# Sparse attention with two expert layers: attention's outputs without an f32 copy, two early weight pieces in place of eight, and the late leaky ReLU on two engines

## Chip, cores, metric

One core of a Trainium2 chip runs the whole program as one launch. The metric is the device time of a launch in microseconds, the median of several runs.

## What is computed

Three layers follow one another (batch 4, 8 heads, 576 positions, head size 64; 2304 tokens of 512 values):

```python
def _attn_ref(q, k, v):             # window 32; heads 4 to 7 dilated by 4
    scores = scale * np.matmul(q, k.transpose(0, 1, 3, 2))
    scores = np.where(masks[None], scores, -1e9)
    attn = np.exp(scores - np.max(scores, axis=-1, keepdims=True))
    attn = attn / (np.sum(attn, axis=-1, keepdims=True) + 1e-09)
    return np.matmul(attn, v)
def _moe_ref(x, w_in, w_out, alpha):   # 512 -> 2048 -> 512, w_in and w_out given as float64
    h = x @ w_in
    g = np.maximum(h, 0.0) + alpha * np.minimum(h, 0.0)
    return g @ w_out
def _moe2_ref(x, w_gate, w1, w2):      # 8 experts, 512 -> 1024 -> 512
    P = ...                            # exp of the gate's logits, 8 Sinkhorn rounds
    for e in range(E):
        out += P[:, e:e+1] * (np.maximum(x @ w1[e], 0.0) @ w2[e])
```

## The kernel before

**Numbers in two parts.** Nearly every matmul works on a value split into a high part (rounded to the matmul's f32r form) and a low part (value minus high part); `three` (lines 377 to 380) gives three matmuls: high with high, high with low, low with high. The splitting of every operand costs an ACT cast for the high part and a subtraction on DVE or POOL for the low one.

**Attention** (`att_S`, `att_E`, `att_R`, `att_X`, `att_V`) works through 16 groups, four to a batch, one group two heads. The sequence of the first four is written out by hand in `opening()`; `attention()` yields the later ones step by step. `att_V` puts the group's result, in PSUM bank `pv`, into the token tile `XS`: ACT casts the high part (line 271, or 282 for the dilated heads), ACT copies the same columns as f32 to `xst` (272, 284), and DVE subtracts for the low part (`low_part`, line 146, emitted later by `flush`). Then SyncE stores `xst` to a DRAM tile `x32[b]` (lines 275 and 287; groups 0 and 1 of a batch pass both lines). After it, `after()` issues the load of v for the group two further on. All DMAs go out on SyncE's queue, in order.

**The first expert layer, plain part.** A unit is 288 tokens (chunk c) by 256 hidden columns; `run` merges the first layer of one unit (`m1_L1`) with the second layer of the unit before (`m1_L2`). `m1_L1` leaves a column tile in PSUM; the leaky ReLU is two DVE instructions (lines 396 and 399), then ACT casts (400) and POOL subtracts (401). Two side lists are stepped between them by credit: `aside` for attention, `wside` for the conversion of weights. Nine units run so (`units[:hand]`).

**Weights from float64.** `from_double` (512 columns a piece) makes f32 values out of the two words of a float64: an absolute value on ACT (521), five DVE instructions (522, 526, 530, 532, 536), then POOL. Eight of the pieces which the *fast* part needs first are converted in this early stage (`early`, EARLY = 8, from unit 4 on, EARLY_AT) and stored to DRAM tiles `wd`.

**The planned part.** `second` lists operations with their engines, costs and due times, and `arrange` plans them: at each time the engine takes the ready operation with the earliest due time, and the due time of an operation is pulled ahead of all those that wait for it. The outcome is a fixed order on each engine. It begins with seven plain units; then the first expert layer's other 1536 hidden columns follow in 12 fast blocks (v = 0 to 11; a batch of tokens by 512 columns, seven products of block matrices in place of eight for layer one, `m1_layer1`; `m1_layer2` for the second). Then the gate, Sinkhorn, and the second expert layer.

- `m1_tokens(b)` makes the four sums T1 to T4 of a batch's tokens: it loads `x32[b]` (line 1200) into a `raw` slot, forms the sums by adds, and splits them into `x` slots.
- `m1_weights(v0)` makes the weights' sums for one column block: for the first block (fi = 1) it loads the `wd` pieces (lines 1144 and 1153); for the later ones it loads the float64 words and calls `double`, the planner's form of the conversion, six DVE instructions with PSUM bank SW[1] as scratch (1080, 1089, 1098, 1105, 1114 and an add).
- The strips of `XS` that hold a batch's tokens are handed to other uses by `release` once their readers are done (`strip_place`); a release has due time 0, so what must come before it is planned early. The strip b12 of batch 0 becomes a place for hidden values (class "h").
- The leaky ReLU in this part runs on two engines: ACT makes relu(-x) (1020, 1284), DVE joins it with `rest` = 1 - alpha (1013, 1279).

Of the kernel before, what the change touches and what calls it, by code (L numbers as in the profile page):

```python
# [58 lines left out]
def program(tc, qk, v, moe_w_in, moe_w_out, moe_alpha, moe2_w_gate, moe2_w1, moe2_w2, masks, out):  # L59
# [8 lines left out]
    x32 = [spill.tile([P, KD, 2 * CH], F32, name=f"x32b{b}") for b in range(B)]  # L68
# [36 lines left out]
    xst = attc.tile([P, 2, 2 * CH], F32, name="xst")  # L105
# [142 lines left out]
    def att_V(i):  # L248
# [6 lines left out]
        for g in range(2):  # L255
# [11 lines left out]
            if g == 0:  # L267
                whole = xst[:, i % 2]
            if p < 2:
                c = 2 * b + g  # L270
                nc.scalar.copy(xh(c, p), pv[:, :CH])
                nc.scalar.copy(whole[:, g * CH : (g + 1) * CH], pv[:, :CH])
                low_part(nc.vector, xl(c, p), pv[:, :CH], xh(c, p))
                if g:
                    nc.sync.dma_start(x32[b][:, p], whole)
                continue
            for cc in range(2):
# [6 lines left out]
            nc.scalar.copy(  # L284
                whole.rearrange("p (j r) -> p r j", r=4)[:, 2 * g : 2 * g + 2], pv[:, :CH].rearrange("p (r j) -> p r j", r=2)
            )
        nc.sync.dma_start(x32[b][:, p], whole)
# [84 lines left out]
    made = [0]  # L372

# [8 lines left out]
    def m1_L1(n, c, st):  # L382
        ah, al = wa_of[n]
        for t in range(FS // P):
            ps = bank("psH")
            cols = slice(t * P, (t + 1) * P)
            for kk in range(KD):
                three(
                    ps[:, :CH], ah[:, kk, cols], al[:, kk, cols], xh(c, kk), xl(c, kk), kk == 0, kk == KD - 1
                )  # L390
            ft = st * (FS // P) + t
            k = made[0]
            made[0] += 1
            gh, gl = gview(k % 4)
            u = GU[:, k % 2]
            nc.vector.tensor_scalar(
                out=u, in0=ps[:, :CH], scalar1=0.0, scalar2=alpha[:, ft : ft + 1], op0=ALU.min, op1=ALU.mult
            )
            nc.vector.scalar_tensor_tensor(out=u, in0=ps[:, :CH], scalar=0.0, in1=u, op0=ALU.max, op1=ALU.add)
            nc.scalar.copy(gh, u)  # L400
            nc.gpsimd.tensor_tensor(out=gl, in0=u, in1=f(gh), op=ALU.subtract)
            gt[c, st, t] = (gh, gl)
            yield
# [58 lines left out]
    EARLY = 8  # L462
# [86 lines left out]
    class Side:  # L549
# [5 lines left out]
        def add(self, g, steps, due):  # L555
            self.q.append([g, steps, due])
# [242 lines left out]
    def second(last, plain):  # L799
# [42 lines left out]
        def dma(kb):  # L842
            return [("SP", kb / 290.0)]
# [111 lines left out]
        def strip_place(b, n):  # L955
            plan = (("h", 1), ("h", NF - 1), ("x", 2), ("x", 3))[b]
            if b > 1 and n != "b12":
                plan = ("zz", 0)
            x = XS[:, 8 * 2 * CH * b : 8 * 2 * CH * (b + 1)].rearrange("p (t h k w) -> p t h k w", t=2, h=2, k=2)
            return Place(lambda: x[:, int(n[2]) - 1, :, int(n[1]) - 1], [plan], block_done[b])  # L960
# [226 lines left out]
        def m1_tokens(b, prio):  # L1187
# [8 lines left out]
            for n in ("T2", "T3", "T1", "T4"):  # L1196
                xo[b, n] = Slot("x", (n, b), b)
            add(
                dma(1180),
                lambda _: nc.sync.dma_start(rawv(r)[:, : KD * 2 * CH].rearrange("p (k c) -> p k c", k=KD), x32[b]),  # L1200
                prio - 15,
                (),
                [(r, i) for i in range(4)],
            )
# [734 lines left out]
        before = last  # L1939
        release([("xs", 0, "b12")], 0, [strip_place(0, "b12")])  # L1940
        m1_tokens(0, TF - 20)
        m1_weights(0, TF - 25, sF(1))
        for i, unit in enumerate(plain):
# [13 lines left out]
        for v in range(NF):  # L1957
            b = batch(v)
            if v < B - 1:
                m1_tokens(v + 1, sF(v + 1) - 15)  # L1960
# [46 lines left out]
    with tc.manual_schedule():  # L2007
# [22 lines left out]
        EARLY_AT = 4  # L2030
# [101 lines left out]
```

## Time and profile before

| | us |
|---|---|
| median of 3 runs | 1990.39 (1990.17 to 1993.63) |
| the profiled execution | 1992.63 |
| its span, first to last instruction | 1990.9 |
| TensorE busy | 1939.9 (97%) |
| VectorE (DVE) busy | 1449.8 (73%) |
| ScalarE (ACT) busy | 1031.5 (52%) |
| GpSimd (POOL) busy | 549.7 (28%) |

The profile is of one execution; its page gives shares over the whole span, so the stages, which have different limits, are read from tables by stretch, from the timeline of an engine, and from the list of what each engine waited for. SPq is SyncE's queue, which issues the DMAs. The granted clock is a mean over a stretch, as a share of 2.4 GHz.

### The profile page before, as it was taken

The page shows a single profiled execution, that of the slowest core. Times are in us where ns is not written, and L with a number is a line of the kernel's source. Part 1 is how long each engine was busy: PE and PEld are TensorE (multiplying, and loading weights), DVE is VectorE, ACT ScalarE, POOL GpSimd, SP SyncE. Part 2 cuts the span into 40 slices and gives each one's busy share as a digit, 9 for nine tenths or more (in the row PEclk, how much of TensorE's full clock was granted, in tenths as well). Part 3 has the DMA queues.
Part 4 walks back from the last instruction along what each step waited for, and adds up shares of the span by engine and source line. Part 5 has one row for each costly group of instructions (what it writes and reads, how often), then busy time and mean ns, then how long its engine had stood idle before and what let it go on. Part 6 is the DMA issues. An engine that isn't in the chain of part 4 may idle for free.

```text
span 1990.9 us, 36935 instructions
## 1 busy us (share of the span) xinstructions
PE 1939.9 (97%) x14629; PEld 1912.9 (96%) x14629; DVE 1449.8 (73%) x2223; ACT 1031.5 (52%) x1915; POOL 549.7 (28%) x413
## 2 busy tenths in 40 slices
PE   6888989999999999999999999999999999999999
PEld 5777989999999999999999999999999999999998
DVE  5686588644657788887967778867776667767776
ACT  6754667666754555645546445534444434444442
POOL 3443253111236545454622112412110101101100
PEclk7998999999999999999999999999999999999999
DMA  7545563718565577867588668677678766666662
GB/s 256 172 144 207 210 221 126 258 54 277 187 215 213 199 256 255 290 244 278 219 329 284 238 207 319 230 285 238 232 272 298 245 209 223 236 212 224 235 214 87
DMA packets 126749, 452.75 MB, mean 227 GB/s; under 512 B 13936, under 2 KB 23920, under 8 KB 121072
## 3 DMA queue, kind: packets, MB, share of 16 engines
q1 hardware_dynamic: 126576, 450.39, 64.9%
q8 instruction: 115, 1.88, 0.4%
q14 instruction: 58, 0.48, 0.1%
HBM read 313.50 MB, written 136.84 MB: 226 GB/s over the span
## 4 chain that ended last, share of the span: by engine, by line
PE 91%; DVE 4%; DMA 2%; ACT 1%; issue 0%; SPq 0%; DVEq 0%; ACTq 0%
PE W L378 8%; PE W L380 8%; PE W L379 8%; PE SW L380 8%; PE SW L379 8%; PE SW L378 8%; PE SX L380 7%; PE SX L378 7%; PE SX L379 7%; PE X L380 6%; PE X L378 6%; PE X L379 6%; PE psS L189 1%; DMA RAW<-in_moe_w_out 1%; PE psV L260 1%; DMA v<-in_v 1%
## 5 line engine op out<-in xcount | busy, mean ns | idle before, releaser
L378 PE MATMUL W<-XS,WT 128*128 128x384 f32 (+1 forms) x936 | 308.2, 329 | 1.5 <-DVE acc L422 0.6
L380 PE MATMUL W<-XS,WT 128*128 128x384 f32 (+1 forms) x936 | 307.2, 328 | 1.3 <-DVE WT L593 1.3
L379 PE MATMUL W<-XS,WT 128*128 128x384 f32 (+1 forms) x936 | 307.3, 328 | 0.0
L1889 DVE SCALAR_TENSOR_TENSOR oR<-SW,pt,oR 128x256 f32<-128x256 f32 x363 | 170.0, 479 | 121.3 <-PE SW L380 119.6
L1889 DVE SCALAR_TENSOR_TENSOR oR<-SX,pt,oR 128x256 f32<-128x256 f32 x351 | 167.6, 480 | 80.9 <-PE SX L380 80.5
L380 PE MATMUL X<-XS,WT 128*128 128x384 f32 (+1 forms) x660 | 218.4, 331 | 0.8 <-DVE WT L593 0.8
L378 PE MATMUL X<-XS,WT 128*128 128x384 f32 (+1 forms) x660 | 218.6, 331 | 0.0
L379 PE MATMUL X<-XS,WT 128*128 128x384 f32 (+1 forms) x660 | 218.2, 331 | 0.0
L378 PEld LDWEIGHTS W<-XS,WT 128*128 128x128 f32 x936 | 176.2, 188 | 2.7 <-DVE acc L422 0.9
L380 PEld LDWEIGHTS W<-XS,WT 128*128 128x128 f32 x936 | 175.7, 188 | 1.6 <-DVE WT L593 1.6
L379 PEld LDWEIGHTS W<-XS,WT 128*128 128x128 f32 x936 | 175.9, 188 | 0.0
L593 POOL TENSOR_TENSOR WT<-rawR,WT 128x512 fp32r<-128x512 f32 (+1 forms) x60 | 79.6, 1332 | 251.5 <-ACT WT L1555 165.5
L593 POOL TENSOR_TENSOR WT<-RAW,WT 128x512 fp32r<-128x512 f32 (+1 forms) x57 | 78.0, 1370 | 257.2 <-ACT WT L1555 113.5
L1679 ACT CAST hR<-WX 128x768 fp32r<-128x768 f32 x127 | 104.3, 834 | 74.8 <-DVE WX L1755 65.9
L593 DVE TENSOR_TENSOR hR<-WX,hR 128x768 fp32r<-128x768 f32 x126 | 141.2, 1129 | 1.9 <-ACT hR L1679 1.7
L593 DVE TENSOR_TENSOR XS<-WX,XS 128x768 fp32r<-128x768 f32 (+1 forms) x117 | 122.5, 1048 | 18.6 <-ACT XS L1286 18.3
L593 POOL TENSOR_TENSOR wR<-rawR,wR 128x512 fp32r<-128x512 f32 x39 | 53.2, 1365 | 269.5 <-ACT wR L1555 154.7
L380 PEld LDWEIGHTS X<-XS,WT 128*128 128x128 f32 x660 | 123.9, 188 | 1.7 <-DVE WT L593 1.5
L378 PEld LDWEIGHTS X<-XS,WT 128*128 128x128 f32 x660 | 124.1, 188 | 0.2
L379 PEld LDWEIGHTS X<-XS,WT 128*128 128x128 f32 x660 | 124.0, 188 | 0.0
L1745 ACT ACTIVATE WX<-WX 128x768 f32<-128x768 f32 x48 | 40.6, 847 | 155.1 <-DVE WX L593 155.1
L593 POOL TENSOR_TENSOR wR<-RAW,wR 128x512 fp32r<-128x512 f32 x39 | 52.6, 1351 | 243.8 <-ACT wR L1555 156.7
(337 smaller groups left out, 6352.3 us busy)
## 6 DMA issues: line engine op xcount, KB each, us to landing
RAW<-in_moe_w SPq DMA_DIRECT2D x20, 1024.0 KB, 6.6
rawR<-in_moe_w SPq DMA_DIRECT2D x19, 1024.0 KB, 6.3
WT<-a11g SPq DMA_DIRECT2D x33, 512.0 KB, 4.5
WT<-S2g SPq DMA_DIRECT2D x33, 512.0 KB, 4.5
WT<-a12g SPq DMA_DIRECT2D x33, 512.0 KB, 3.7
WT<-S3g SPq DMA_DIRECT2D x33, 512.0 KB, 3.5
WT<-S1g SPq DMA_DIRECT2D x33, 512.0 KB, 3.6
WT<-a22g SPq DMA_DIRECT2D x33, 512.0 KB, 4.9
```

Source lines behind the costliest of these rows:

```text
L189: nc.tensor.matmul(ps[half(hh), bk, at : at + KB], x[half(hh), 0, j * QB : (j + 1) * QB], x[half(hh), 1, key_start(j) : key_start(j) + KB] ...
L260: nc.tensor.matmul(pv[half(hh), lo - g * CH : hi - g * CH], vt[:, j, hh * D : (hh + 1) * D], at[:, j, hh * QB + lo - j * QB : hh * QB + hi ...
L378: nc.tensor.matmul(ps, lh, rh, start=start, stop=False, skip_group_check=more)
L379: nc.tensor.matmul(ps, lh, rl, start=False, stop=False, skip_group_check=more)
L380: nc.tensor.matmul(ps, ll, rh, start=False, stop=stop, skip_group_check=more)
L593: eng.tensor_tensor(out=out, in0=x, in1=y, op=op)
L1679: add(act(n2), lambda _: nc.scalar.copy(hv(h[n])[:, 0], tm[i]), prio, [("t", i)], [(h[n], "h")])
L1745: add(act(n2), lambda _: nc.scalar.activation(tm[1], tm[1], AF.Relu), t + 1, [("t", 1)], [("t", 1)])
L1889: nc.vector.scalar_tensor_tensor(out=o, in0=x, scalar=p_, in1=o, op0=ALU.mult, op1=ALU.add)
```

## The change

- `att_V` no longer copies the result as f32 and no longer stores it; the tiles `xst` and `x32` are gone.
- `m1_tokens` rebuilds a batch's tokens as high part plus low part, four adds (on DVE or POOL) from `XS` into the `raw` slot, in place of the load. It is called for all batches ahead of the plain units (batch 0 still first); the release of batch 0's strip b12 moves behind batch 0's, and that strip first serves the class "x" (token sums of era 0), then "h" as before.
- EARLY is 2, not 8, and the early pieces begin at unit 6, not 4. The six others are converted by `double` in the planned part: two of the first matrix, all four of the second.
- From the ninth column tile on (BUSY = 8, so from unit 4), `m1_L1`'s leaky ReLU is relu(-x) on ACT and one join on DVE.

```diff
@@ att_V
-            if g == 0:
-                whole = xst[:, i % 2]
             if p < 2:
                 c = 2 * b + g
                 nc.scalar.copy(xh(c, p), pv[:, :CH])
-                nc.scalar.copy(whole[:, g * CH : (g + 1) * CH], pv[:, :CH])
                 low_part(nc.vector, xl(c, p), pv[:, :CH], xh(c, p))
-                if g:
-                    nc.sync.dma_start(x32[b][:, p], whole)
                 continue
...
                 nc.scalar.copy(ho, src)
                 low_part(nc.vector, lo, src, ho)
-            nc.scalar.copy(
-                whole.rearrange("p (j r) -> p r j", r=4)[:, 2 * g : 2 * g + 2], pv[:, :CH].rearrange("p (r j) -> p r j", r=2)
-            )
-        nc.sync.dma_start(x32[b][:, p], whole)
@@ m1_L1
+            if k < BUSY:
                 ...
+            else:
+                nc.scalar.activation(u, ps[:, :CH], AF.Relu, scale=-1.0)
+                nc.vector.scalar_tensor_tensor(
+                    out=u, in0=u, scalar=rest[:, ft : ft + 1], in1=ps[:, :CH], op0=ALU.mult, op1=ALU.add
+                )
@@
-    EARLY = 8
+    EARLY = 2
@@ strip_place
+            plan = [plan]
+            if (b, n) == (0, "b12"):
+                plan = [("x", 0), *plan]
@@ m1_tokens
-            add(
-                dma(1180),
-                lambda _: nc.sync.dma_start(rawv(r)[:, : KD * 2 * CH].rearrange("p (k c) -> p k c", k=KD), x32[b]),
-                prio - 15,
-                (),
-                [(r, i) for i in range(4)],
-            )
+            for i, n in enumerate(("b11", "b12", "b21", "b22")):
+                x = xs_view(b, n)
+                add(
+                    flex(n2),
+                    lambda e, i=i, x=x: sub(E3[e], blk(i), f(x[:, 0]), f(x[:, 1]), ALU.add),
+                    prio - 2,
+                    [("xs", b, n)],
+                    [(r, i)],
+                )
@@ second
+        m1_tokens(0, TF - 20)
         release([("xs", 0, "b12")], 0, [strip_place(0, "b12")])
-        m1_tokens(0, TF - 20)
         m1_weights(0, TF - 25, sF(1))
+        for b in range(1, B):
+            m1_tokens(b, sF(b) - 15)
...
-            if v < B - 1:
-                m1_tokens(v + 1, sF(v + 1) - 15)
@@
-        EARLY_AT = 4
+        EARLY_AT = 6
```

## Rows read from the trace of the kernel before

**Rows 1.** The page: busy time of TensorE, and its granted clock in forty slices.

```profile
PE 1939.9 (97%) x14629; PEld 1912.9 (96%) x14629; DVE 1449.8 (73%) x2223; ACT 1031.5 (52%) x1915; POOL 549.7 (28%) x413
...
PEclk7998999999999999999999999999999999999999
```

**Rows 2.** Table by stretch: length, busy PE, PEld, DVE, ACT, POOL, clock, DMA share, GB/s.

```profile
20.00:52.00 32.00, 23.47 (x311) 19.61 (x312) 19.88 (x42) 21.67 (x87) 10.14 (x7) 0.69 0.63 210
52.00:124.00 72.00, 68.24 (x918) 60.86 (x917) 53.99 (x108) 49.10 (x154) 33.15 (x26) 0.98 0.53 170
124.00:190.40 66.40, 51.34 (x452) 46.44 (x446) 52.35 (x98) 31.86 (x89) 26.72 (x21) 0.82 0.46 149
190.40:234.00 43.60, 43.57 (x328) 43.57 (x329) 20.59 (x37) 23.64 (x57) 12.20 (x11) 1.00 0.57 212
234.00:258.70 24.70, 18.52 (x132) 17.38 (x131) 20.31 (x31) 15.88 (x31) 9.38 (x6) 0.99 0.72 271
```

**Rows 3.** Timeline of TensorE: start, length, instruction, idle time before and its releaser.

```profile
171.42 0.40 PE L378 MATMUL psY<-GP,WT 128*128 128x288 f32 x1 [2.52 <-DVE GU L399]
...
177.37 0.44 PE L380 MATMUL psY<-GP,WT 128*128 128x288 f32 x1
```

**Rows 4.** Groups on DVE, 124 to 190 us: count, busy us, mean ns, idle before.

```profile
L536 DVE SCALAR_TENSOR_TENSOR RAW<-RAW 128x512 f32<-128x512 uint32 x9 | 6.2, 686 | 0.2
...
L396 DVE TENSOR_SCALAR GU<-psH,alpha 128x288 f32<-128x288 f32 x8 | 4.1, 513 | 3.0 <-PE psH L380 3.0
L399 DVE SCALAR_TENSOR_TENSOR GU<-psH,GU 128x288 f32<-128x288 f32 x8 | 3.7, 458 | 0.3
```

**Rows 5.** Groups on ACT, 0 to 190 us.

```profile
L284 ACT COPY xst<-psV 128x288 f32<-128x288 f32 x16 | 11.9, 745 | 0.0
```

**Rows 6.** Groups on DVE, 0 to 190 us.

```profile
L146 DVE TENSOR_TENSOR XS<-psV,XS 128x144 fp32r<-128x144 f32 x32 | 11.7, 415 | 14.6 <-ACT xst L284 14.6
```

**Rows 7.** Timeline of all engines, 33 to 47 us.

```profile
37.61 1.29 ACT L237 COPY at<-psX 96x512 f32<-96x512 f32 x3
...
37.84 0.33 SPq L287 DMA_DIRECT2D x32b<-xst  x1
...
38.26 0.39 SPq L132 DMA_DIRECT2D v<-in_v  x1
...
42.77 2.40 PE L260 MATMUL psV<-at,v 96*64 96x64 f32 x40 [4.63 <-DMA v<-in_v]
```

**Rows 8.** Instructions on tile WX alone, 126.5 to 186 us: DVE, ACT, POOL.

```profile
126.50:186.00 59.50, 23.60 (x32) 5.45 (x8) 11.58 (x9) 0.83 0.47 151
```

**Rows 9.** Groups on DVE, 186 to 262 us.

```profile
L1013 DVE SCALAR_TENSOR_TENSOR WX<-WX,rest,W 128x288 f32<-128x288 f32 x7 | 3.6, 513 | 8.9 <-ACT WX L1020 8.9
```

**Rows 10.** Groups on DVE, 255 to 400 us; then line 1080: ns, first and last start.

```profile
L1114 DVE SCALAR_TENSOR_TENSOR RAW<-RAW,MIDF 128x512 f32<-128x512 uint32 x16 | 12.8, 800 | 0.3
...
L1080 DVE TENSOR_SCALAR SW<-RAW 128x512 uint32<-128x512 uint32 x16 | 11.1, 692 | 0.4
...
L1080 DVE TENSOR_SCALAR SW<-RAW x16: 681/695/697, 260.1 to 373.8; 128x512 uint32<-128x512 uint32 x16
```

**Rows 11.** Timelines of SyncE's queue and of DVE behind 190 us.

```profile
203.55 1.28 SPq L1200 DMA_DIRECT2D MIDF<-x32b  x1
...
219.80 1.11 DVE L593 TENSOR_TENSOR MIDF<-MIDF 128x576 f32<-128x576 f32 x1
```

**Rows 12.** Timelines of TensorE, DVE and POOL, 246 to 258 us.

```profile
257.43 0.40 PE L379 MATMUL SW<-XS,WT 128*128 128x288 f32 x1 [4.38 <-DVE XS L593]
...
251.68 3.15 DVE L1279 SCALAR_TENSOR_TENSOR WX<-WX,rest 128x288 f32<-128x288 f32 x2
...
251.49 4.60 POOL L593 TENSOR_TENSOR MIDF<-MIDF 128x576 f32<-128x576 f32 x3
```

**Rows 13.** Adds of 128x576: on DVE (255 to 400 us), on POOL (186 to 262 us).

```profile
L593 DVE TENSOR_TENSOR MIDF<-MIDF 128x576 f32<-128x576 f32 x4 | 3.0, 750 | 0.0
...
L593 POOL TENSOR_TENSOR MIDF<-MIDF 128x576 f32<-128x576 f32 x6 | 9.2, 1540 | 7.7 <-PE W L380 6.9 <-DVE MIDF L593 0.7
```

More of the change, by code (lines that the diff above doesn't have):

```diff
@@ L67, in program @@
     spill = pool(es, "spill", space=bass.MemoryType.DRAM)
-    x32 = [spill.tile([P, KD, 2 * CH], F32, name=f"x32b{b}") for b in range(B)]
     py = pool(sp, "py", bufs=2, space=PSUM)
@@ L104, in program @@
     eye = attc.tile([P, P], BF16, name="eye")
-    xst = attc.tile([P, 2, 2 * CH], F32, name="xst")
     def load_consts():
@@ L372, in program @@
     made = [0]
+    BUSY = 8
     def gview(k):
@@ L395, in m1_L1 @@
             u = GU[:, k % 2]
-            nc.vector.tensor_scalar(
-                out=u, in0=ps[:, :CH], scalar1=0.0, scalar2=alpha[:, ft : ft + 1], op0=ALU.min, op1=ALU.mult
-            )
-            nc.vector.scalar_tensor_tensor(out=u, in0=ps[:, :CH], scalar=0.0, in1=u, op0=ALU.max, op1=ALU.add)
+            if k < BUSY:
+                nc.vector.tensor_scalar(
+                    out=u, in0=ps[:, :CH], scalar1=0.0, scalar2=alpha[:, ft : ft + 1], op0=ALU.min, op1=ALU.mult
+                )
+                nc.vector.scalar_tensor_tensor(out=u, in0=ps[:, :CH], scalar=0.0, in1=u, op0=ALU.max, op1=ALU.add)
+            else:
[3 more added lines that the diff above has]
+                )
             nc.scalar.copy(gh, u)
@@ L958, in strip_place @@
                 plan = ("zz", 0)
+            plan = [plan]
+            if (b, n) == (0, "b12"):
+                plan = [("x", 0), *plan]
             x = XS[:, 8 * 2 * CH * b : 8 * 2 * CH * (b + 1)].rearrange("p (t h k w) -> p t h k w", t=2, h=2, k=2)
-            return Place(lambda: x[:, int(n[2]) - 1, :, int(n[1]) - 1], [plan], block_done[b])
+            return Place(lambda: x[:, int(n[2]) - 1, :, int(n[1]) - 1], plan, block_done[b])
         def wt_place(i, cls):
@@ L1197, in m1_tokens @@
                 xo[b, n] = Slot("x", (n, b), b)
-            add(
-                dma(1180),
-                lambda _: nc.sync.dma_start(rawv(r)[:, : KD * 2 * CH].rearrange("p (k c) -> p k c", k=KD), x32[b]),
-                prio - 15,
-                (),
-                [(r, i) for i in range(4)],
-            )
+            for i, n in enumerate(("b11", "b12", "b21", "b22")):
[6 more added lines that the diff above has]
+                    [(r, i)],
+                )
             def total(at, x, y):
```

## Prediction

> **What bounds the kernel now.** The page's busy shares come first: TensorE is busy 1939.9 us of the span, 97%, so about 51 us is all that idling costs, and its clock row is below 9 only in the first slices [rows 1]. What a change outside TensorE's own work can win therefore lies early. The table by stretches says where [rows 2]: from 20 to 52 us TensorE is busy 23.47 of 32.00 at a granted clock of 0.69, from 52 to 124 us 68.24 of 72.00, from 124 to 190.4 us only 51.34 of 66.40 at 0.82, then, the work having been handed over to the planned order, 43.57 of 43.60, and from 234 to 258.7 us 18.52 of 24.70. Behind that I expect nothing of these edits.
>
> Idle time has a second price, the clock. After the wait of 2.52 us that ended at 171.42, a 128x288 matmul at 177.37 still shows 0.44 us, the form of the lower level, 1.2 GHz [rows 3]. A mean of 0.82 between the levels 1 and 0.5 means 36% of the 66.4 us, 24 us, at the lower one; half of that, 12 us, is lost work, some 2 us of it while TensorE idled anyway: 10 us. With the idle 66.4 - 51.3 = 15.1 us, TensorE's own work in that stretch is 66.4 - 15.1 - 10 = 41.3 us.
>
> What it waits for there is DVE, busy 52.35 of the 66.40 us [rows 2]. Its groups are the conversion of the weight pieces (lines 522 to 536) and the leaky ReLU (396 and 399) [rows 4]. DVE works in order: a piece that waits for its words to land holds up the ReLU behind it, and the wait at 171.42 us ends on line 399 [rows 3].
>
> **The change part by part.**
>
> *No f32 copy, up to 124 us.* It removes 32 ACT copies (the longer half 0.745 us each, overlapped, so about 0.5 us of the queue) [rows 5] and 24 stores of 288 KB. DVE stood idle 14.6 us before the low parts (line 146), and what ended it was the copy of line 284, not the cast that they need [rows 6]. On SyncE's queue the second store of group 1 went at 37.84 us; it writes the place that the first one writes. The load of v for group 3, ready to go when its buffer was free at about 32 us, stood behind it and went at 38.26; TensorE waited for it 4.63 us, until 42.77 [rows 7]. Without the stores it lands 4.5 us after 32, at 36.5, and what is late next is ACT's copy of at, which began at 37.61 and took 1.29 [rows 7], less some 1.5 us for the copies ahead of it: 37.5. Gain 5.2 us. Two more copies stand before the next exponentials, 0.5 us each: 1 us. Of the 3.8 us that TensorE idles from 52 to 124 us a quarter: 1 us. Sum 7 us; at least 4 (the load alone, less what the next wait takes), at most 10 (if 3 us of the slow clock after that wait go too).
>
> *Two early pieces, not eight, 124 to 190 us.* The eight cost DVE 23.60 us in lines 522 to 532 [rows 8] and 8 x 0.686 in line 536 [rows 4], 29.1 us; six are 21.8. *Late ReLU*: units 4 to 8 hold ten column tiles; each pair of 0.513 + 0.458 us [rows 4] becomes one join, in the form of line 1013 0.513 us [rows 9]: 4.6 us less on DVE, against ten more instructions on ACT, about what it loses in copies; it is busy 31.86 of 66.40 us [rows 2]. The ReLU on ACT waits for TensorE's columns, and exponentials and casts queue behind it; till now the cast of the same columns stood there one step later, so I put it at nothing; without that cover some 0.4 us a tile, 4 us. DVE's demand falls to 52.4 - 21.8 - 4.6 = 26 us, under TensorE's 41.3. What ends last is then TensorE with the small waits that it has where attention and the layers are mixed and no early piece runs, 68.24 of 72.00: 41.3 / 0.95 = 43.5, with one slow stretch of 6 us, a quarter of the 24 (3 us lost), and 2 us around the two pieces that stay 48.5 us. Gain 18 us; at least 11 (the waits on DVE go, three slow stretches stay), at most 23.
>
> *The moved conversions, from the hand-over on* (T0 = 190.4 us). In the planner's form a conversion has six DVE instructions, five of about 0.69 us (that of line 1080 has 0.692) and line 1114 with 0.800 [rows 10]: 4.26 us, 25.6 for six, one absolute value on ACT each and a load of 512 KB in place of 256. Twelve stores of tokens go ahead of all loads on SyncE; the first load behind them went at 203.55 us, and the first preparation on DVE came at 219.80, T0 + 29.4 [rows 11]. That load, of 1152 KB, is gone now. DVE had 20.59 of 43.60 us of work up to 234 us [rows 2], so the two pieces of the first matrix fit: done at T0 + 38 back to back, at T0 + 45 at the pace that the sixteen later ones show (first at 260.1, last at 373.8 us: 7.6 us apart) [rows 10]. The fast layer begins at T0 + 44; a matmul is 43.57 / 328 = 0.133 us, a product 12 of them, 1.6 us, and the third product needs the second of these pieces: late by 2 us at most. The four of the second matrix follow, done at T0 + 55 back to back, T0 + 75 at the slow pace. The first fast second layer was ready at T0 + 63 and went on at 257.43 us, T0 + 67, after 4.38 us for a low part [rows 12]. Bounds: 6 us gained (the idle 24.7 - 18.5 us goes and nothing new comes), or 14 lost (8 us later, a slow stretch of 3, another wait of 3). I take 4 lost, nearer to the slow pace than to back to back because DVE is also given the adds below. Behind it there is slack: half of the sixteen serve blocks that begin eight times 180 matmuls after T0 + 44, near 425 us, and are done by 378; that is 34 us of DVE work that can wait.
>
> *Tokens rebuilt.* Sixteen adds of 128x576, 0.750 us on DVE or 1.540 on POOL [rows 13], 12 to 25 us, for four loads. They read what is resident, and as the release of the strips waits for them they are given the earliest due time; the first block's go into idle time of DVE and POOL behind T0, the second's take the place of a load. Nothing of their own in the sum; if all fall on DVE's path, 12 us, the worse end above. The strip that held hidden values from the start first holds a token sum, last read by the sixth product and wanted back after the seventh: nothing.
>
> The two engines do hold each other up: two joins at 251.68 us took 3.15 us while POOL ran three adds in 4.60 [rows 12]; single joins have 0.51 [rows 9]. The Trainium skill (SBUF — State Buffer, "Who interferes with whom") has it that a DVE instruction with two SBUF inputs and a GpSimd instruction that reads SBUF exclude each other for the whole instruction. The trace agrees; by that rule the sixteen adds could take up to 16 x 1.54 = 25 us from the two engines, and the sum would come to 4 us slower, not 21 faster.
>
> **Sum**, against the profiled execution (1992.63 us, span 1990.9): -7 - 18 + 4 = -21, 1971.6. The median shown is 2.24 us below that execution: 1969.4 us.
>
> **The rivals.**
> 1. *Half or more comes back* (gain 4 to 14 us, about 1981): the hand-over loses 14 us in place of 4, or three slow stretches stay before it. For it: DVE has 20.31 of 24.70 us of work from 234 us on [rows 2]. Against it: the slack named above.
> 2. *Slower than before*: the second matrix comes too late because DVE and POOL hold each other up ahead of it, as at 251.68 us. Six conversions at 7.6 us end 46 us after the first begins; seven products of the next block, 11 us, can cover. The 25 us gained are lost when that end is past T0 + 67 + 25 + 11 = T0 + 103, so from a first conversion after T0 + 57: 27 us later than the first preparation now. Sixteen adds that each cost 1.54 us ahead of it would do that. Some 1996 us. Against it: DVE's 23 idle us up to T0 + 44.
> 3. *More* (over 29 us): no new wait behind the hand-over: 1992.63 - 10 - 21 - 4 - 2.24, about 1955.
> 4. *Nothing* (within 0.2%): ACT with its added ReLU holds TensorE from 124 to 190 us as DVE does now. Its 32 busy us speak against it.
>
> **How the numbers follow.** Forecast (gain 14 to 29 us) 0.59, rival 1 0.15, rival 2 0.09, rival 3 0.12, rival 4 0.05. 0.2% is 4 us, about what a measurement of this kernel can tell from no change. Faster 0.59 + 0.15 + 0.12 = 0.86, same 0.05, slower 0.09. The range leaves out rivals 2 and 4 and the far end of 3: 1957 to 1984.
>
> **What would show it.** The hand-over at 163 to 168 us; group 3's value matmul near 37.5 us; no wait on the ReLU's join over 1.5 us; the first fast second layer 62 to 75 us after the hand-over; from the hand-over to the end 1795 to 1815 us (1800.5 now). Wrong if the hand-over moves by less than 12 us, or if TensorE idles over 16 us in the 80 us behind it.

## The result and the profile after

| | before | after |
|---|---|---|
| median, runs side by side | 1991.36 (1990.17 to 1993.63) | 1966.48 (1965.82 to 1967.32) |
| profiled execution, span | 1992.63, 1990.9 | 1966.24, 1964.4 |

All times here are in us. The ratio is 0.9874 (95% interval 0.9857 to 0.9891), a gain of 24.9 us; 1969.4 was forecast, with a range of 1957 to 1984. So the total was right. It was right partly because two terms of the sum failed in opposite directions, which the experiments show below. The two profiled executions lie 26.4 us apart, more than the medians, because that of the kernel before was a long one; the terms read from traces below add up to this larger difference.

The page of the changed kernel, busy time and granted clock, answers to [rows 1]:

```profile
PE 1922.2 (98%) x14629; PEld 1899.1 (97%) x14629; DVE 1453.1 (74%) x2214; ACT 1025.1 (52%) x1893; POOL 568.9 (29%) x428
...
PEclk9999999999999999999999999999999999999999
```

TensorE runs as many matmuls as before, 14629, and is busy 17.7 us less. A matmul at the lower clock counts as longer busy, so the lost clock shows up as busy time; the clock row, in which no slice is below 9 any more, shows where that went. DVE's sum has hardly moved: its work was not removed but placed elsewhere.

The table by stretch, after; columns as in [rows 2]: length, busy PE, PEld, DVE, ACT, POOL, clock, DMA share, GB/s. The hand-over, the first matmul of the planned order, is now at 159.46 us:

```profile
20.00:52.00 32.00, 25.35 (x386) 21.56 (x386) 26.68 (x56) 23.41 (x94) 13.82 (x11) 0.95 0.61 196
52.00:124.00 72.00, 67.13 (x908) 60.84 (x908) 50.73 (x105) 48.52 (x149) 32.52 (x26) 0.98 0.42 129
124.00:159.46 35.46, 33.13 (x387) 30.85 (x386) 22.78 (x49) 21.13 (x60) 13.12 (x12) 1.00 0.18 59
159.46:190.00 30.54, 30.54 (x230) 30.54 (x231) 25.03 (x39) 16.39 (x40) 12.34 (x10) 1.00 0.94 342
190.00:220.00 30.00, 28.90 (x216) 28.46 (x215) 26.66 (x43) 21.75 (x47) 22.62 (x18) 1.00 0.16 54
220.00:231.50 11.50, 3.59 (x17) 3.31 (x16) 11.23 (x15) 3.84 (x6) 10.15 (x9) 0.70 0.52 201
```

From 124 us to the hand-over TensorE is busy 33.13 of 35.46 us at a clock of 1.00, where it had 51.34 of 66.40 at 0.82. The last line is the worst stretch behind the hand-over: 11.5 us in which TensorE works 3.59, and DVE 11.23.

**Cutting the run at common events.** Stretches with the same clock times hold different work in two kernels, so all kernels below are cut at two events that each of them has: the start of the last attention group's scores, and the hand-over. The rows of TensorE's timeline, before (whose hand-over is at 190.43); the first row is the start of group 14's scores, the second that of the last group's:

```profile
120.23 0.54 PE L176 MATMUL psS<-mk,eye 128*128 128x480 bf16 x2
...
138.04 0.54 PE L176 MATMUL psS<-mk,eye 128*128 128x480 bf16 x2
...
190.43 0.40 PE L378 MATMUL W<-XS,WT 128*128 128x288 f32 x1 [0.55 <-DVE acc L422]
```

and after:

```profile
111.18 0.54 PE L174 MATMUL psS<-mk,eye 128*128 128x480 bf16 x2
...
125.31 0.54 PE L174 MATMUL psS<-mk,eye 128*128 128x480 bf16 x2
...
159.46 0.40 PE L368 MATMUL W<-XS,WT 128*128 128x288 f32 x1 [0.55 <-DVE acc L418]
```

This gives three terms: the opening (to the last group) 138.04 to 125.31, a gain of 12.7; the middle (last group to hand-over) 52.4 to 34.15, a gain of 18.2; the rest (hand-over to the end of the span) 1800.5 to 1804.9, a loss of 4.4. Together that is 26.5, the difference of the two spans. The forecast parted its first two terms at 124 us, which is nearer to group 14's scores; cut there, the gains are 9.05, 21.9 and -4.4.

**The opening.** The timelines of SyncE's queue and of all engines after, around group 3's value matmul, answer to [rows 7]:

```profile
29.47 0.33 SPq L130 DMA_DIRECT2D v<-in_v  x1
...
36.52 0.75 ACT L235 COPY at<-psX 96x512 f32<-96x512 f32 x2 [0.22 <-PE psX L234]
36.63 1.34 PEld L258 LDWEIGHTS psV<-at,v 96*64 96x64 f32 x40 [0.36 <-ACT at L235]
36.63 1.48 PE L258 MATMUL psV<-at,v 96*64 96x64 f32 x40
```

The load of v for group 3 goes out at 29.47, as soon as group 1's value matmul (28.04 to 29.43) has freed its buffer, in place of 38.26, and group 3's value matmul starts at 36.63 in place of 42.77. What ends its short wait of 0.36 us is ACT's copy of at, as forecast.

**Behind the hand-over.** Timelines of DVE, POOL, ACT and TensorE after, in order of the chain that holds TensorE:

```profile
218.64 2.79 POOL L589 TENSOR_TENSOR MID<-MIDF,MID 128x576 fp32r<-128x576 f32 x2
221.40 1.60 POOL L589 TENSOR_TENSOR GP<-WX,GP 128x576 fp32r<-128x576 f32 x1
...
219.40 0.94 DVE L1280 SCALAR_TENSOR_TENSOR WX<-WX,rest,X 128x288 f32<-128x288 f32 x2 [0.66 <-ACT WX L1285]
220.25 3.06 DVE L1280 SCALAR_TENSOR_TENSOR WX<-WX,rest 128x288 f32<-128x288 f32 x2
...
223.35 0.67 ACT L1287 CAST XS<-WX 128x576 fp32r<-128x576 f32 x1 [2.26 <-DVE WX L1280]
...
224.10 1.41 POOL L589 TENSOR_TENSOR XS<-WX,XS 128x576 fp32r<-128x576 f32 x1 [1.10 <-ACT XS L1287]
...
225.54 0.65 ACT L1285 ACTIVATE WX<-W 128x576 f32<-128x576 f32 x1 [0.24 <-POOL XS L589]
...
227.48 0.93 DVE L1280 SCALAR_TENSOR_TENSOR WX<-WX,rest,W 128x288 f32<-128x288 f32 x2
...
228.56 0.58 PE L368 MATMUL W<-XS,WT 128*128 128x288 f32 x1 [7.91 <-DVE WX L1280]
```

The next product of a first layer wants PSUM bank W, which the leaky ReLU's join has to read first; that join stands behind the joins of another quarter of the hidden values, a cast and a low part, and on DVE behind four instructions of the fifth conversion (from 224.68). TensorE waits 7.91 us, and the matmul that ends the wait shows 0.58 us, not 0.40: the granted clock of 220 to 231.5 us is 0.70, between the level 2.4 GHz (1) and 1.2 GHz (0.5). No second layer is planned in the gap: the first one comes at 241.46, 82.0 us after the hand-over (61.5 before, 251.96), since its weights are not converted until 238.77. DVE's line of the conversions between 180 and 242 us, and SyncE's queue ahead of them:

```profile
L1079 DVE TENSOR_SCALAR SW<-RAW x7: 684/687/699, 187.8 to 239.5; 128x512 uint32<-128x512 uint32 x7
```

```profile
170.78 1.98 SPq L1233 DMA_DIRECT2D b22b<-XS  x1
172.81 1.27 SPq L1072 DMA_DIRECT2D RAW<-in_moe_w_in  x1
```

The first load of float64 words goes at 172.81, right behind the last of the twelve token stores, and the first conversion starts at 187.8, 28.3 us after the hand-over.

### The profile page after: what moved, and what is told of

Same layout as the page of the kernel before. It is cut to its first block, busy times and chain, and to the rows that moved or that the text cites. A ratio compares the mean times of both kernels' runs of the same rounds, so it can differ in the third digit from the quotient of the medians.

```text
span 1964.4 us, 36831 instructions
## 1 busy us (share of the span) xinstructions
PE 1922.2 (98%) x14629; PEld 1899.1 (97%) x14629; DVE 1453.1 (74%) x2214; ACT 1025.1 (52%) x1893; POOL 568.9 (29%) x428
## 4 chain that ended last, share of the span: by engine, by line
PE 94%; DVE 2%; ACT 1%; DMA 1%; POOL 1%; issue 0%; SPq 0%; POOLq 0%; DVEq 0%; ACTq 0%
PE W L368 8%; PE W L370 8%; PE W L369 8%; PE SW L370 8%; PE SW L369 8%; PE SW L368 8%; PE SX L370 8%; PE SX L368 7%; PE SX L369 7%; PE X L368 6%; PE X L370 6%; PE X L369 6%; PE psS L187 1%; PE psV L258 1%; DMA mk<-in_masks 1%; PE psX L241 0%
```

## The experiments

Each kernel is cut at the two events named above. "2nd layer" is the first fast second layer's start after the hand-over. The span is that of the profiled execution; medians of different sessions differ by up to 0.12% for the same kernel (1989.11 to 1991.36 us for the kernel before), so the ratio to the kernel before of the same session stands beside them.

| kernel | median | ratio | opening | middle | rest | 2nd layer |
|---|---|---|---|---|---|---|
| before | 1990.4 | 1 | 138.04 | 52.4 | 1800.5 | 61.5 |
| after | 1966.5 | 0.9874 | 125.31 | 34.15 | 1804.9 | 82.0 |
| copies_back | 1981.3 | 0.9955 | 134.88 | 34.4 | 1810.5 | 82.1 |
| copies_gone_alone | 1979.7 | 0.9943 | 126.10 | 49.6 | 1803.1 | 63.4 |
| eight_early | 1976.6 | 0.9930 | 124.28 | 47.75 | 1802.5 | 63.3 |
| six_early | 1968.9 | 0.9886 | 122.87 | 38.2 | 1805.2 | 78.1 |
| four_early | 1972.7 | 0.9907 | 125.34 | 38.1 | 1807.5 | 61.5 |
| four_from_unit_4 | 1972.6 | 0.9913 | 125.83 | 37.95 | 1807.3 | 61.5 |
| relu_on_dve | 1967.4 | 0.9883 | 126.50 | 34.3 | 1804.7 | 82.1 |
| rebuild_on_dve | 1968.9 | 0.9889 | 126.22 | 34.15 | 1807.7 | 86 |
| inner_loads_first | 1966.7 | 0.9886 | 122.73 | 34.15 | 1804.8 | 62.5 |
| stores_later | 1965.1 | 0.9877 | 126.02 | 34.15 | 1803.2 | 62.4 |
| later_and_on_dve | 1961.1 | 0.9861 | 123.89 | 34.1 | 1801.1 | 61.6 |
| one_store | 1986.2 | 0.9983 | 130.24 | 51.7 | 1800.8 | 61.2 |

The eleven kernels without copies, which share their opening, reach the last group between 122.73 and 126.50 us: the opening of one profiled execution is known to some 2 us either way. The middle is far steadier: five kernels that differ only behind the hand-over have 34.1 to 34.15. The rest is steady too: kernels whose planned parts are the same differ by 0.2 to 0.6 us in it (before and one_store; after and relu_on_dve; eight_early and copies_gone_alone; the two with four pieces). So a hand-over by itself tells little of an edit worth 2 us; the middle and the rest do. One caution holds for the rest: every edit that touches the planned part makes the planner order all engines anew, so such a run changes more than the edit names.

**copies_back: the pieces and the ReLU alone.** The kernel before with two lines of settings and the two-engine ReLU (its branch, left out here, is that of the change):

```diff
+    BUSY = 8
...
-    EARLY = 8
+    EARLY = 2
...
-        EARLY_AT = 4
+        EARLY_AT = 6
```

> The kernel before with two early pieces from unit 6 and the late ReLU on two engines, but with the f32 copies, the stores and the loads of the tokens as they were. Theory (copies and stores cost 7 us in the opening and 2 us up to 124 us): the group-5 scores start at 45.1 us (38.0 in the changed kernel), the hand-over comes 9 to 11 us later than 159.5; behind it the tokens wait for their loads but there are no rebuilt adds: 1800 to 1806 us from the hand-over on; median 1973 to 1979 us. Rival (the rebuilt adds cost more behind the hand-over than the copies in front): below 1970 us.

Measured: 1981.28 (1980.91 to 1982.82), and 1810.5 behind the hand-over, both above what was expected. It splits the change in two. Pieces and ReLU, from before to here: opening 3.2 gained (1.4 of it by group 7's scores, 60.40 and 59.00, long before a piece starts, so that much is no work of the pieces), middle 18.0 gained, rest 10.0 lost. Copies, stores and loads, from here to after: opening 9.6, middle 0.3, rest 5.6, all gained. TensorE's row at group 3's value matmul is that of before, with the same releaser (timeline of TensorE, copies_back):

```profile
42.93 2.40 PE L260 MATMUL psV<-at,v 96*64 96x64 f32 x40 [5.91 <-DMA v<-in_v]
```

**one_store: the write that comes twice.** The kernel before, with the second of two stores to the same place left out:

```diff
             if p < 2:
...
                 low_part(nc.vector, xl(c, p), pv[:, :CH], xh(c, p))
-                if g:
-                    nc.sync.dma_start(x32[b][:, p], whole)
                 continue
```

> The kernel before without the first of the two stores that groups 0 and 1 of a batch issue (line 275); the copies and the other store stay. Theory (the second store waits for the first because both write one place, and the load of v stands behind it on SyncE's queue): the load of v for group 3 goes at about 34 us in place of 38.3, group 3's value matmul starts at 38.9 us in place of 42.8, limited by ACT's copy of at; 3 to 5 us faster, about 1986.5 us. Rival (the load waits for its buffer or for bandwidth): it goes at 37 to 38 us as before, and the time stays at 1990 us.

Measured: ratio 0.9983 (0.9972 to 0.9994) over ten runs, 1986.19 (1983.33 to 1990.25). Timeline of SyncE's queue and TensorE, one_store:

```profile
32.51 0.33 SPq L285 DMA_DIRECT2D x32b<-xst  x1
32.93 0.39 SPq L132 DMA_DIRECT2D v<-in_v  x1
...
37.03 2.40 PE L260 MATMUL psV<-at,v 96*64 96x64 f32 x40 [0.58 <-DVE XS L146]
```

Group 1's store, the only one now, is not held up, the load of v for group 3 goes right behind it, at 32.93 in place of 38.26, the wait of 4.63 us for v is gone, and the value matmul starts at 37.03 (38.9 was expected), near that of the changed kernel (36.63), with all f32 copies still on ACT and all other stores still on SyncE. Group 5's scores begin at 39.36 in place of 45.10. Of these 5.7 us 0.8 stand already at group 4's scores (26.88 and 27.69), ahead of any effect of the store; so some 5 us of the opening's gain come from the repeated store in front of a load, and not from the copies. In the total, by the ratio, it is 3.4 us, with an interval of 1.2 to 5.6.

**eight_early and copies_gone_alone: the middle, term by term.** The changed kernel with eight early pieces from unit 4, and the same with the ReLU on DVE alone too:

```diff
-    EARLY = 2
+    EARLY = 8
-        EARLY_AT = 6
+        EARLY_AT = 4
```

and, in copies_gone_alone alone, where the ReLU's two instructions so stay on DVE:

```diff
-    BUSY = 8
+    BUSY = 100
```

> The changed kernel, but with eight early pieces from unit 4 on; the copies stay gone and the late ReLU stays on two engines. Theory (the six pieces are what held DVE between 124 us and the hand-over): the hand-over, at 159.5 us in the changed kernel and 190.4 before, comes back to 172 to 180 us, with waits of 2 us and more on DVE in front of the second layer's matmuls; what follows the hand-over shortens by the 4 us that it grew; median 1975 to 1982 us. Rival (the ReLU on two engines freed DVE, the pieces hide): hand-over at 160 to 164 us, median 1966 us or below, since the planned part has 25 us less for DVE.

> The changed kernel with eight early pieces from unit 4 and the ReLU on DVE alone: of the change only the copies, stores and loads are gone. Theory (with eight pieces DVE is the bound ahead of the hand-over, so the 4.6 us that the ReLU adds to it count there, though they cost only 1.3 with two pieces): hand-over 3 to 6 us later than the 172.0 of eight pieces with the late ReLU on two engines, median 1980 to 1983 us. Rival (the ReLU on two engines is worth nothing in either): 172 to 173.5 us, 1977 us.

Measured: 1976.59 (1975.76 to 1977.12) and 1979.68 (1978.52 to 1981.64). The middle goes 52.4, 49.6 without the copies, 47.75 with the ReLU on two engines, 34.15 with two pieces: 2.8, 1.9 and 13.6 us. How eight pieces hold TensorE stands in eight_early's timelines of DVE, POOL and TensorE:

```profile
146.60 0.43 DVE L518 TENSOR_SCALAR WX<-RAW 128x512 uint32<-128x512 uint32 x1 [1.98 <-DMA RAW<-in_moe_w_out]
...
151.64 1.86 DVE L518 TENSOR_SCALAR WX<-RAW 128x512 uint32<-128x512 uint32 x1
...
151.26 1.96 POOL L223 TENSOR_TENSOR s<-s,rs 128x864 f32<-128x864 f32 x1 [0.36 <-DVE rs L222]
...
156.46 0.61 PE L368 MATMUL psY<-GP,WT 128*128 128x288 f32 x1 [2.00 <-DVE GU L393]
```

DVE stands still for 1.98 us until a piece's words land, with the ReLU queued behind, and an instruction of 0.43 us takes 1.86 where POOL works too; TensorE's wait ends on the ReLU's join (line 393), and the matmul then shows 0.61 us, the lower clock. It is the mechanism of [rows 3], seen again.

**relu_on_dve.** The changed kernel with `BUSY = 100` in place of 8.

> The changed kernel with the leaky ReLU of all column tiles as two DVE instructions again. Theory: DVE has slack once the six pieces are gone (26 us of work under 41 us of TensorE's), so 4.6 us more on it cost little: hand-over 0 to 3 us later than 159.5 us, median 1966 to 1970 us. Rival (the ReLU is worth its full 4.6 us and the clock behind it): hand-over 5 to 9 us later, 1971 to 1975 us.

Measured: 1967.43 (1964.97 to 1968.8), the middle 34.3 against 34.15. With two pieces the ReLU's move is worth 0.15 us; with eight it was 1.9. Here, work that DVE sheds is worth something only as long as DVE is what ends last.

**four_early, four_from_unit_4, six_early: what a piece costs.** `EARLY = 4` from unit 6, `EARLY = 4` from unit 4, `EARLY = 6` from unit 4.

> The changed kernel with four early pieces (all of the first matrix), from unit 6; only the second matrix's four are converted behind the hand-over. Theory (the 7.9 us wait of TensorE 69 us behind the hand-over comes from the six conversions in DVE's order: the first fast second layer can't start before the last of them, 82 us behind the hand-over, and the first layer of two blocks has to run without it): two conversions less bring the first fast second layer to 62 to 70 us behind the hand-over, the wait falls under 3 us, 1797 to 1801 us from the hand-over to the end (1804.9 now); the hand-over itself comes 1 to 4 us later than 159.5; median 1960 to 1965 us. Rival (a piece costs its 2 us ahead of the hand-over and nothing behind it): median 1970 us.

> The changed kernel with four early pieces from unit 4 on (four from unit 6 brought the hand-over from 159.5 to 163.5 us, six from unit 4 only to 161.1). Theory (ahead of the hand-over a piece costs nothing as long as DVE fits under TensorE in every unit; what costs is crowding pieces into few units): hand-over at 159.5 to 161 us; behind it 1804 to 1808 us as with four from unit 6. Rival (a price of 2 us a piece): hand-over at 163.5 us again.

> The changed kernel with six early pieces, from unit 4. Theory: DVE becomes the bound ahead of the hand-over again, which comes 6 to 9 us later than 159.5; behind it 1798 to 1802 us; median 1966 to 1971 us, between four and eight pieces. Rival (a piece costs the same ahead and behind): 1966 us with the hand-over at 168.

Measured: 1972.66, 1972.61 and 1968.94 (1965.27 to 1970.2). With two, four, six and eight pieces the middle is 34.15, 38.1, 38.2, 47.75: steps of 4, 0 and 9.6 us, not the even price that six times the same DVE work would suggest. Idle time alone is less uneven, 2.33, 4.39, 5.28 and 10.54 us of the middle; the clock adds to it with four pieces (0.96) and eight (0.89), and not with two and six (1.00). Where four pieces begin makes no difference, against the theory of four_from_unit_4. six_early's hand-over came 1.6 us later, not 6 to 9, and its rest is 1805.2, not 1798 to 1802, so that its median met the theory by luck. four_early's theory failed too: the second layer is back at 61.5 us, but the rest is 1807.5, not 1797 to 1801, for the wait has only moved: it now stands in the second layer, for a weight piece (timelines of ACT and TensorE, four_early):

```profile
233.70 0.62 ACT L1130 CAST WT<-MIDF 128x512 fp32r<-128x512 f32 x1 [0.66 <-DVE MIDF L589]
...
234.37 0.61 PE L368 MATMUL SW<-GP,WT 128*128 128x288 f32 x1 [6.13 <-ACT WT L1130]
```

**rebuild_on_dve: do DVE and POOL hold each other up?** The sixteen rebuilding adds on DVE alone:

```diff
-                    flex(n2),
+                    dve2(n2),
                     lambda e, i=i, x=x: sub(E3[e], blk(i), f(x[:, 0]), f(x[:, 1]), ALU.add),
```

> The changed kernel with the sixteen rebuilding adds on DVE only, none on POOL. Theory (the 7.9 us wait is set by the order of the conversions, not by DVE and POOL holding each other up): the wait stays at 6 us or more, median 1965 to 1969 us. Rival (the adds on POOL hold DVE up, 2.98 us for two adds at 214.41 and 3.06 us for two joins at 220.25 behind the hand-over): the joins take 0.94 us again, the wait falls under 4 us, median 1960 to 1963 us.

Measured: 1968.88 (1967.8 to 1970.2); rest 1807.7 against 1804.9. The edit moved less than its name says: in the changed kernel the planner had already put thirteen of the sixteen adds on DVE, and three on POOL (213.5, 214.8 and 231.2 us). Timelines of POOL, DVE and TensorE, rebuild_on_dve:

```profile
219.03 3.30 POOL L589 TENSOR_TENSOR MID<-MIDF,MID 128x576 fp32r<-128x576 f32 x2
...
222.50 0.94 DVE L1280 SCALAR_TENSOR_TENSOR WX<-WX,rest 128x288 f32<-128x288 f32 x2
...
221.08 0.40 PE L368 MATMUL W<-XS,WT 128*128 128x288 f32 x1 [2.07 <-DVE W L589]
...
228.67 0.58 PE L368 MATMUL W<-XS,WT 128*128 128x288 f32 x1 [5.45 <-DVE WX L1280]
```

The two joins that took 3.06 us beside POOL take 0.94. What had stood beside them there were low parts (218.64 and 221.40), not the rebuilding adds; here POOL's low parts end at 222.33, just before the joins begin. And yet TensorE waits 2.07 and 5.45, together 7.52, where the changed kernel has 0.71 and 7.91. In both the second layer is late, and DVE's queue is no shorter.

**inner_loads_first and stores_later: the twelve stores.** Two ways to let the first loads of weight words leave ahead of the token stores. The first pulls the loads' due time forward:

```diff
+            if o.rush:
+                o.prio -= 100
...
             add(dma(512), load, prio - 15, (), [U_, L_])
+            ops[-1].rush = st < 4
...
+                    ops[-1].rush = True
```

The second gives each store of an inner token part a due time just ahead of its reader, not that of the strip's release:

```diff
+            if o.own is not None:
+                o.prio = o.own
...
                     [("xm", b, n)],
                 )
+                ops[-1].own = sF(b) - 10
```

> The changed kernel with the loads for the first fast block ahead of the twelve stores; only two float64 pieces fit in their place at once, so the second matrix's loads still follow the stores. Theory (start of the conversions): the first two come 10 to 20 us earlier than 28 us behind the hand-over, the four others only a few us earlier; 1801 to 1805 us behind the hand-over, median 1962 to 1967 us, between the changed kernel and the run with all stores later. Rival (DVE's sum): 1804 to 1806 us, as the changed kernel.

> The changed kernel with the twelve stores of tokens behind the hand-over due when their block is, not with the release that waits for them, so that the loads of the six moved pieces go between them on SyncE's queue. Theory (the 10 us that TensorE idles 50 to 80 us behind the hand-over come from DVE's queue being full there, and the conversions start only 28 us behind the hand-over because their loads stand behind the stores, while DVE has 1 to 4 idle us in each 10 from 20 us on): the first conversion starts 8 to 20 us behind the hand-over, the first fast second layer at 62 to 75 in place of 82 us, idle time from the hand-over to 300 us falls from 11 us to 4 to 8, 1798 to 1803 us from the hand-over to the end; median 1960 to 1965 us. Rival (DVE's sum of work sets it, wherever the conversions stand): 1804 to 1806 us behind the hand-over, median 1966 us.

Measured: 1966.65 (1963.51 to 1969.71) and 1965.10 (1963.84 to 1965.51). In inner_loads_first the first conversion starts at 161.81 us, 4.9 after the hand-over, and the second layer comes at 62.5, and yet the rest is 1804.8, as in the changed kernel: the longest wait, 3.34 us, is now one of the second layer for a weight piece, as in four_early. In stores_later the loads and stores alternate, and the conversions start at 165.10 in place of 187.79, earlier than the theory had it (timelines of SyncE's queue, DVE, POOL and TensorE, stores_later):

```profile
157.41 0.37 SPq L1075 DMA_DIRECT2D RAW<-in_moe_w_in  x1
157.83 0.60 SPq L1236 DMA_DIRECT2D b11b<-XS  x1
...
165.10 0.68 DVE L1082 TENSOR_SCALAR SW<-RAW 128x512 uint32<-128x512 uint32 x1
...
222.89 2.77 POOL L589 TENSOR_TENSOR MIDF<-MIDF 128x576 f32<-128x576 f32 x2
...
224.27 2.13 DVE L1284 SCALAR_TENSOR_TENSOR WX<-WX,rest 128x288 f32<-128x288 f32 x2
...
225.95 0.40 PE L368 MATMUL SW<-GP,WT 128*128 128x288 f32 x1 [2.38 <-ACT GP L1291]
...
227.13 0.61 PE L369 MATMUL SW<-GP,WT 128*128 128x288 f32 x1 [0.78 <-DVE GP L589]
```

The wait of 7.91 us is gone and the second layer is at 62.4, yet only 1.7 us of the rest are won: two waits of 2.38 and 0.78 us and the lower clock behind them come at nearly the same place, and DVE's joins stand beside POOL's work again (token sums; only one of the sixteen rebuilding adds is on POOL, at 194.2). TensorE idles 5.0 us less than in the changed kernel (5.40 against 10.44 in the 110 us behind the hand-over). The clock takes most of that back: in the changed kernel it is low where TensorE stands still (0.51 from 224.46 to 229.46 us, busy 0.90), in stores_later where it works (0.61 and 0.71 in the two 5 us from 225.17 on, busy 8.44 of 10).

**later_and_on_dve.** Both edits, stores_later and rebuild_on_dve, together, to tell what is left: the two engines holding each other up, or simply DVE's queue. Against stores_later the second edit moves a single add; the rest of the difference is the new order that the planner makes of it.

> The changed kernel with two edits: stores of the inner tokens due just ahead of their reader, so that the first loads of weight words leave before them (as in stores_later), and the sixteen rebuilding adds on DVE alone (as in rebuild_on_dve). In stores_later the conversions began 22 us earlier than in the changed kernel and the wait of 7.9 us was gone, but TensorE still waited 2.38 and 0.78 us at 225.95 and 227.13, and POOL's two rebuilding adds (222.89 us, 2.77 us) stood beside two joins of 2.13 us on DVE. Theory A (a full DVE queue sets this, not the two engines holding each other up): the joins fall to about 0.95 us, but the adds lengthen DVE's queue by about as much; a wait of 2 to 5 us stays near the third block's first layer, hand-over to end 1802 to 1806 us, total 1963 to 1967. Rival B (the hold-up between DVE and POOL is what is left): both waits fall under 0.5 us, no 0.5 clock near 228 us, hand-over to end 1798 to 1800 us, total about 1960.

Measured: ratio 0.9861 (0.9845 to 0.9878), 1961.11 (1959.62 to 1962.44). Timelines of DVE and TensorE:

```profile
225.48 0.93 DVE L1284 SCALAR_TENSOR_TENSOR WX<-WX,rest 128x288 f32<-128x288 f32 x2
...
220.79 0.40 PE L368 MATMUL SW<-GP,WT 128*128 128x288 f32 x1 [0.26 <-ACT GP L1291]
...
222.99 0.40 PE L369 MATMUL SW<-GP,WT 128*128 128x288 f32 x1 [1.80 <-POOL GP L589]
```

The rest is 1801.1, 3.8 us better than after and just below what theory A gave (1802 to 1806), above rival B's 1798 to 1800; the joins are at 0.93, the waits 0.26 and 1.80, and a short stretch at a clock of 0.73 (225 to 230 us) stays. Neither theory is confirmed. Alone, the first edit gains 1.7 us of the rest and the second loses 2.8; together they gain 3.8. That a late second layer hides what the hold-up costs would fit this, but it is not shown: the edit moves one add at 194.2 us, and what slowed the joins in stores_later were POOL's token sums at 222.89, which the edit doesn't name and which the new order merely puts elsewhere. The total is the lowest of all kernels here, though its interval of the ratio overlaps that of after.

## Why the prediction came out right, and where it was wrong

**The opening, 7 predicted (4 to 10).** The change gained 9.05 us up to group 14's scores (120.23 to 111.18), 12.7 up to the last group's. By copies_back against after, 7.7 up to group 14's scores (118.86 to 111.18) belong to copies and stores, 9.6 up to the last group's, both within the range; the remaining 1.4 to 3.2 are no more than what the opening varies by. The step itself held, place and size: the load of v behind the repeated store was named at 5.2 us, one_store measured about 5; the value matmul was forecast for 37.5 and came at 36.63. The term I had kept only as the far end, a clock that does not fall, came true: 0.95 from 20 to 52 us against 0.69.

**The middle, 18 predicted (11 to 23).** 18.2 by the cut at the last group. That the numbers meet is luck of the cut: at group 14's scores, near the 124 us of the forecast, the gain is 21.9, still within the range. What carried it was the pieces (13.6 of 18.2), as forecast; no wait on the ReLU's join shows among TensorE's waits from 124 us to the hand-over, the longest being 0.9 us for ACT's copy of acc. Two terms of the 48.5 us were not needed: I kept 3 us for one slow stretch and 2 us around the two pieces that stay; the clock was 1.00 throughout, and from the counterpart of 124 us (3.77 us behind group 14's scores) to the hand-over it took 44.5, near the 43.5 of the sum without them. The ReLU's 4.6 us stood only in DVE's demand, which is under TensorE's 41.3 with them or without; relu_on_dve bears that out with 0.15, while with eight pieces they were worth 1.9. The linear view, so many instructions times so many ns, overstates the second of two reliefs on one engine. The hand-over, forecast for 163 to 168, came at 159.46, because the opening gave 2 us more and this stretch 4.

**The moved conversions, 4 predicted (-6 to 14): the step that failed, with its size hidden.** After lost 4.4 us behind the hand-over, the number forecast, but not by its mechanism. The forecast put the first fast second layer at 62 to 75 us after the hand-over with a low part ending late; it came at 82. The first start was right, T0 + 28.3 against the T0 + 29.4 of [rows 11]. The pace was a little slower: the seven starts from 187.8 to 239.5 us are 8.6 apart, not 7.6, so that the sixth piece is through DVE at 238.8, T0 + 79, beyond the slow end of T0 + 75. The larger failure is the step from "the weights are ready" to "TensorE waits": I let the third block's first layers run on while the pieces were late, and priced only the lateness of the second layer. In this planned order the late second layer leaves first layers back to back, and these wait for each other's PSUM bank through the join, 7.91 us plus a clock of 0.70. This is the form that the lateness takes here, not the only one: with the second layer early, in four_early and inner_loads_first, the wait stands in the second layer and the rest is 1807.5 and 1804.8. copies_back measures the term by itself, with the tokens loaded as before: the rest loses 10.0 us, 2.5 times the forecast, inside its bounds. Little of it is more idle time (9.63 us in the 110 us behind the hand-over, 6.18 before); the clock is 0.53 from 234 to 249 us, where TensorE is busy 9.96 of 15 us.

**Tokens rebuilt: nothing predicted, 5.6 gained.** The rest of copies_back is 1810.5, of after 1804.9: with conversions late, sixteen adds (thirteen on DVE, three on POOL) are better than four loads of 1152 KB by 5.6 us. That cancels most of the 6 us by which the term before it was too small. With eight pieces the same edit costs 2.6 (1800.5 to 1803.1). So the two terms cannot be added in either order, and a forecast term by term was right here by two errors of opposite sign. What exactly the loads delay in copies_back, the queue or the strips' release, no run here separates.

**The rivals.** Rival 4 (ACT would hold TensorE) fell: no wait of TensorE in the middle ends on the ReLU's ACT half. Rival 3 (over 29 us) fell with the new wait behind the hand-over. Rival 2 (slower) asked for a first conversion after T0 + 57; it came at T0 + 28.3. Rival 1 asked for 14 us lost behind the hand-over; 4.4 were lost, and 10.0 where the tokens are still loaded. The hold-up between DVE and POOL is real in the rows: two joins of a sum that lies in SBUF took 3.06 us beside POOL's low parts and 0.94 without them. The Trainium skill (SBUF — State Buffer, "Who interferes with whom") has it for a DVE instruction with two SBUF inputs beside a GpSimd instruction that reads SBUF. The trace agrees, also in that the two joins at 219.40, whose second input is in PSUM, took 0.94 beside the same low parts. By that rule the prediction had the sum at 4 us slower, and 24.9 faster was measured: thirteen of the sixteen adds went to DVE, and the moves of the other three and of one (rebuild_on_dve, later_and_on_dve) came with a new order each, so what the hold-up costs the total is not shown.

**The markers.** TensorE idles 10.4 us (busy 69.56) in the 80 us behind the hand-over, most of it the one wait of 7.91; 16 was the bound. The hand-over moved by 31.0 us; 12 was the bound. The rest, 1804.9, lies within 1795 to 1815.

**Still open.** Why the middle takes steps of 4, 0 and 9.6 us with four, six and eight pieces was not followed through the order on DVE. What ends last behind the hand-over once the second layer is early is not shown either. The 2 us that the opening varies by in profiled executions of identical code has no cause shown here.

## What to carry to other kernels

Cut both traces at events that they share, not at clock times, and price each stretch by what ends last in it: relief on an engine that is already off the path is worth nothing (the ReLU, 0.15 us), while one repeated store ahead of a load on an in-order queue held TensorE up by some 5 us. When a step is moved into a fixed order, ask not only when its result is ready but what the waiting engine will run in its place, and which buffer that work needs; here back-to-back first layers waited 7.9 us for one PSUM bank. Count idle time and lost clock apart: 5.0 us less waiting gave back 1.7. And where a planner orders the engines, count in the trace what an edit moved before explaining what it did: "sixteen adds to DVE" moved three in one kernel and one in another, and the order around them changed as well.

## What the runs showed of the hardware that was not expected

A repeated write to one DRAM place, ordered behind the first, holds up all that is queued behind it on SyncE: in the kernel before, the first store of a token part went at 33.48 us, the second one, of the same data, 4.36 us later, and the load of v behind it; TensorE waited 4.63 us. With one store only it waited 0.58 us, for something else. The mutual hold-up of DVE and POOL is large in single instructions and depends on where the inputs lie: beside the same low parts of POOL, two joins of SBUF with SBUF took 3.06 us (0.94 without them), two joins of SBUF with PSUM 0.94. And waits that go need not come back in full: stores_later has 5.0 us less of them and gained 1.7, for its lower clock (0.61 and 0.71) falls on 10 us with 8.44 of work, that of the changed kernel (0.51) on 5 us with 0.90.
